# FNet + PEER kernel: the first stage ordered by hand and pinned, query weights loaded first, the column-257 sums on GpSimd, six statistics on ScalarE

## The chip, the cores and the metric

The kernel runs on one core of one Trainium2 chip. The time is that of the device in microseconds (us), from the runs of the whole program. Matrix work is done by TensorE (PE); VectorE (DVE), ScalarE (ACT) and GpSimd (POOL) work on arrays; SyncE (SP) issues most of the transfers (DMA). Each engine goes through its own list of instructions in order and waits at an instruction until what it needs is there.

## The reference

From one array x (2048 rows, 512 columns) and its normalised rows xn, two things are computed and added to x:

```python
def _A_ref(xn, dft_seq_re, dft_seq_im, dft_hid_re, dft_hid_im):
    a = jnp.einsum("bsd,ed->bse", xn, dft_hid_re)
    b = jnp.einsum("bsd,ed->bse", xn, dft_hid_im)
    return jnp.einsum("ts,bse->bte", dft_seq_re, a) - jnp.einsum("ts,bse->bte", dft_seq_im, b)

def _B_ref(xn, w_q, k1, k2, u, v):        # 32 heads, 64 keys, K = 2, 4096 experts
    q = jnp.einsum("nd,dhc->nhc", xn, w_q)
    s1 = jnp.einsum("nhd,ed->nhe", q[..., :dk], k1)
    s2 = jnp.einsum("nhd,ed->nhe", q[..., dk:], k2)
    ...
    g = _softmax(top_s, axis=-1)
    act = _gelu(jnp.einsum("nd,nhkd->nhk", xn, u[top_e]))
    return jnp.einsum("nhk,nhk,nhkd->nd", g, act, v[top_e])

return x + _A_ref(xn, ...) + _B_ref(xn, ...)
```

A is the real part of a Fourier transform over rows and columns. B takes for each row and head the two best of 64 keys from each of two sets, adds their scores in pairs, keeps the best two of the four sums, and adds up the outputs of the experts chosen in this way. All inputs are float32.

## The kernel before

**Tiles and groups.** The 2048 rows are 16 tiles of 128 rows. Four tiles make a group, which `xp[2 * g]` and `xp[2 * g + 1]` hold (128 x 2 x 512 float32 each, half a megabyte); `xn(g, q)` is one tile. A group consists of the rows that the symmetry of the transform brings together. The groups are taken in the order `G = (1, 0, 2, 3)`.

**What the first stage does with a group.** `ln` collects mean and variance of its four tiles, on DVE (L361 and L362, `bn_stats` and `bn_aggr`) or, for two tiles of the second group and one of the fourth, on ACT with two instructions (L347, L348). A square root on ACT and five or more small instructions on DVE (L367 and its neighbours) make the scale and the shift; `ln_norm` applies them, two tiles on DVE (L313), two on ACT (L386). `fold(k, g)` then adds (k = 0, for the cosines) or subtracts (k = 1, sines) mirrored halves: one instruction over 1024 columns (L416), then some of 254 to 257 columns (L397, L400, L405 to L407, L419, L420), all on DVE but the copy L405. The result, 2 x 257 columns, is `Q[k][g]`. `main(k, g)` multiplies it on PE by the table `A[k, g]` that `load(k, g)` brought (L449, eight records of 512 columns in float32), and adds the four groups up in four banks of PSUM. `stage(i)` splits a normalised tile into a high half on ACT (L521) and a low half on DVE (L522), both 16 bits wide, and SP transposes them by DMA (L523) for the scores.

**Query weights.** The scores need products of the query weights with the keys. The heads are worked on in eight chunks. For a chunk, `m_load` loads four tiles of weights, `m_mul(j, t, kds)` multiplies them by the keys on PE (L152, 64 columns wide), and `m_parts` splits the result for 16-bit products (ACT L226, DVE L227). For the first chunk the scale comes from sums over the weights and keys (`w_sums`, ACT L209 and the next, then one product by ones on PE, then `w_scale`). `early(n)` computes the scores of the first eight tiles for the first chunk inside the first stage (PE L252, 12 products of 512 columns each, ACT L285 takes them out of PSUM).

**What the tiles leave over.** Column 257 of the folded arrays does not fit into the 256 columns of the products. `sides` adds up these parts for all groups on DVE, with one fused multiplication and addition each (L454, L456, L477) at the end of the stage. `fold_row` folds the one row that stands alone, on POOL (L425, then L397 to L407 on one partition); `spread` and `evict` bring the results out of PSUM.

**Order.** The kernel is written as a program in one order, and a planner sorts the instructions of each engine by its own estimates, so that instructions of later work can be put ahead. An instruction given to `tc.keep_in_program_order` stays behind the one that its engine had before it in the text. Nothing in the first stage of this kernel is pinned. `heat(n)` puts n products of ones on PE which nobody uses (L555). `behind_stage` writes one column of a buffer on POOL from a staged tile, so that the load into that buffer waits for that tile (L587). Loads of x, of the tables, of weights and the transposes are issued from SP; `c5s`, `c5r`, `c55` and `x5`, all small, from ACT. The transfers are told apart by eight counters in turn, so the ninth waits for the first.

**Behind the first stage** come the sums over the parts left over (`sums`, POOL L825 to L833, `hid` with POOL L540 and L541), the weights of the next chunks, which `m_prep` splits (ACT L162, POOL L166 and L167), the scores of all tiles, the routing on DVE and POOL, and the experts (PE L1103), which take most of the time.

## Time and profile before

| | |
|---|---|
| median of three runs (lowest, highest) | 1115.78 us (1115.4, 1116.73) |
| profiled execution, its time | 1117.59 us |
| its span, first to last instruction | 1115.7 us |
| mean granted clock of PE | 0.996 |
| PE busy | 1102.7 us, 99% of the span |
| PE loading weights | 721.8 us, 65% |
| DVE busy | 937.7 us, 84% |
| ACT busy | 695.8 us, 62% |
| POOL busy | 333.4 us, 30% |
| instructions | 29227 |

The profile comes from one execution of the program. An engine's time counts as busy while it executes an array instruction; weight loads run beside the products and are counted by themselves. `L152` is line 152 of the kernel. A group of instructions is named by line, engine, operation and tile (`m<-k_sb,wq`: from `k_sb` and `wq` into `m`), with its partitions and elements, its type and count, then the busy time in us, the mean duration of one in ns, and the idle time just before them with what ended it. In the timeline a row has its start in us, its duration in us, then the instruction; a bracket gives how long the engine had waited and for what; `x24` joins so many of a kind in one row. The first stage lasts until about 77 us.

### The profile page before, as it was taken

How to read it: one execution, taken by the hardware profiler on the slowest of the kernel's cores; microseconds unless marked ns; L12 is line 12 of the kernel's file. 1: busy time of each engine (PE TensorE's matmuls, PEld its weight loads, DVE VectorE, ACT ScalarE, POOL GpSimd, SP SyncE). 2: the span in 40 equal slices, each digit the busy share in tenths (PEclk: the TensorE clock that was granted, in tenths of full speed). 3: DMA queues.
4: the chain of work that ended last, by engine and by line, in shares of the span. 5: the costliest groups of instructions: out<-in, count | busy, mean ns of one | idle time of the engine just before them, and what ended most of it. 6: DMA issues, size and time to landing. Idle time of an engine off the chain costs nothing.

```text
span 1115.7 us, 29227 instructions
## 1 busy us (share of the span) xinstructions
PE 1102.7 (99%) x11528; PEld 721.8 (65%) x11528; DVE 937.7 (84%) x2828; ACT 695.8 (62%) x1238; POOL 333.4 (30%) x385
## 2 busy tenths in 40 slices
PE   9999999999999999999999999999999999999997
PEld 6465554545445449877677677677677677677643
DVE  7899698999999899697797797699699599599790
ACT  6557598988887666355665666565657566566520
POOL 1519999898888861000000000000000000000000
PEclk8999999999999999999999999999999999999999
DMA  8885456464362353587678677677768867866433
GB/s 285 259 216 189 133 197 203 139 205 136 114 199 80 101 140 110 168 259 274 242 237 294 236 254 270 228 244 256 255 224 270 300 221 236 294 204 218 134 105 117
DMA packets 134866, 229.96 MB, mean 206 GB/s; under 512 B 35380, under 2 KB 71355, under 8 KB 134718
## 3 DMA queue, kind: packets, MB, share of 16 engines
q1 hardware_dynamic: 132112, 223.72, 60.1%
q0 software_dynamic: 2304, 4.20, 2.2%
q8 instruction: 92, 1.51, 0.6%
q14 instruction: 56, 0.46, 0.1%
q10 hardware_dynamic: 302, 0.08, 0.0%
HBM read 192.49 MB, written 29.69 MB: 199 GB/s over the span
## 4 chain that ended last, share of the span: by engine, by line
PE 80%; DVE 7%; POOL 6%; DMA 3%; ACT 2%; issue 1%; SPq 0%; POOLq 0%; ACTq 0%; DVEq 0%
PE z L1103 27%; PE v L1103 27%; PE s L252 19%; PE g L1103 4%; PE m L148 1%; POOL v L795 1%; DVE L L1098 1%; DVE vals L972 1%; PE m L152 1%; PE p L449 1%; DVE idx L976 1%; DVE g L1098 1%; DMA xt_d<-xq 1%; POOL u L540 1%; POOL v L825 1%
## 5 line engine op out<-in xcount | busy, mean ns | idle before, releaser
L252 PE MATMUL s<-m,xq 128*128 128x512 f16 x1344 | 297.5, 379 | 1.4 <-ACT ss L968 1.4
L1103 PE MATMUL v<-v,act 128*128 128x512 f16 (+1 forms) x1068 | 248.3, 377 | 0.7 <-DVE act L1098 0.7
L252 PEld LDWEIGHTS <-xq 128*128 128x128 f16 x1344 | 129.7, 98 | 152.6 <-issue 2.7
L1385 POOL DMA_DIRECT2D y<-in_x_dram x16 | 14.4, 899 | 647.2 <-DMA y<-y_d 318.4
L1103 PEld LDWEIGHTS <-u 128*128 128x128 f16 x3456 | 198.3, 98 | 14.4
L1103 PEld LDWEIGHTS <-act 128*128 128x128 f16 x1068 | 97.9, 98 | 95.7 <-DVE act L1098 1.2
L1098 DVE TENSOR_TENSOR L<-io_lam,cmp 128x2048 f16<-128x2048 f16 x120 | 144.9, 1220 | 6.9 <-PE g L1103 6.7
L972 DVE MAX8 vals<-ss 128x8 f32<-128x64 f32 x896 | 133.3, 216 | 5.3 <-ACT ss L968 5.1
L1103 PE MATMUL z<-xb,u 128*128 128x128 f16 x2112 | 127.7, 219 | 0.0
L1103 PEld LDWEIGHTS <-s 128*128 128x128 f16 x1944 | 113.4, 98 | 12.5
L1103 PE MATMUL v<-v,w 128*128 128x512 f16 x480 | 113.0, 379 | 0.0
L1098 ACT ACTIVATE cx<-cx 128x896 f32<-128x896 f32 (+2 forms) x134 | 83.5, 625 | 31.7 <-DVE cx L1098 30.3
L968 ACT ACTIVATE ss<-s,wsc 128x512 f32<-128x512 f32 x120 | 80.1, 680 | 22.4 <-PE s L252 12.6
L1098 DVE TENSOR_TENSOR cx<-cx 128x128 f32<-128x128 f32 (+9 forms) x226 | 91.7, 418 | 2.7 <-DMA cx<-in_cb_dram 1.1
L976 DVE FIND_INDEX8 idx<-vals,ss 128x8 uint16<-128x256 f32 x224 | 93.8, 419 | 0.0
L1103 PE MATMUL z<-x,u 128*128 128x128 f16 x1344 | 84.2, 219 | 0.0
L1098 ACT ACTIVATE act<-act,scl 128x512 f32<-128x512 f32 x56 | 40.2, 719 | 66.4 <-DVE act L1098 66.4
L1103 PE MATMUL z<-x,s 128*128 128x128 f16 x1296 | 81.2, 219 | 0.0
L1103 PEld LDWEIGHTS <-L 128*128 128x128 f16 x2048 | 65.0, 96 | 16.1 <-DVE R L1098 0.7
L1098 ACT ACTIVATE act<-g 128x1024 f16<-128x1024 f32 x40 | 51.5, 1311 | 37.3 <-DVE g L1098 36.9
L1098 DVE TENSOR_TENSOR act<-z,act 128x512 f32<-128x512 f32 x44 | 30.4, 690 | 49.7 <-PE z L1103 45.9
L1103 PEld LDWEIGHTS <-w 128*128 128x128 f16 x480 | 43.8, 98 | 43.2
(333 smaller groups left out, 1794.8 us busy)
## 6 DMA issues: line engine op xcount, KB each, us to landing
s<-s_d SPq DMA_DIRECT2D x81, 512.0 KB, 4.4
v<-v_d SPq DMA_DIRECT2D x67, 512.0 KB, 4.7
cx<-in_cb_dram SPq DMA_DIRECT2D x64, 448.0 KB, 5.9
w<-in_wq_dram SPq DMA_DIRECT2D x28, 512.0 KB, 5.9
fit<-in_wq_dram SPq DMA_DIRECT2D x28, 512.0 KB, 5.0
uv<-in_vn_dram SPq DMA_DIRECT2D x16, 512.0 KB
uv<-in_ut_dram SPq DMA_DIRECT2D x16, 512.0 KB, 3.6
s_d<-v SPq DMA_DIRECT2D x32, 256.0 KB, 2.5
```

The source lines that it names most:

```text
L148: nc.tensor.matmul(MS[j, "p"][kd][:, c0:c0 + 64], MS[j, t, "l" if l else "h"][:, hh, kd * P:(kd + 1) * P], k16[:, r, t // 2, :], start=n = ...
L152: nc.tensor.matmul(MS[j, "p"][kd][:, c0:c0 + 64], MS[j, t][:, hh, kd * P:(kd + 1) * P], k_sb[:, t // 2, :], start=True, stop=True)
L252: nc.tensor.matmul(ps, xt[i][:, l, kd, :], m[:, r, kd, :], start=(n == 0), stop=(n == 3 * KD - 1))
L449: nc.tensor.matmul(PP[k][dt][h], l[:, dt * P:(dt + 1) * P], r, start=first, stop=last)
L540: nc.gpsimd.tensor_tensor(t[:, b:513:2], t[:, e], im, op=ALU.add)
L795: nc.gpsimd.tensor_tensor(l, t, h, op=ALU.subtract)
L968: nc.scalar.activation(s, ps, AF.Copy, scale=inv)
L972: nc.vector.max(vals[:, i, w, :, h], s[:, g, :])
L976: nc.vector.max_index(idx[:, i, w].rearrange("p k h -> p (k h)"), vals[:, i, w, 0:2].rearrange("p k h -> p (k h)"), s[:, w * HC:g + 1, :]. ...
L1098: return (lambda *a, **k: pin(f(*a, **k))) if keep_on[0] else f
L1103: i = nc.tensor.matmul(*a, **k)
L1385: pin(nc.gpsimd.dma_start(Y[b], x[b % 4, b // 4], accum_op=ALU.add))
```

## The change

In the first stage every instruction on DVE, ACT, PE and SP is pinned to the order in which the program has it: the four engines are wrapped in `First`, which pins while `keep0[0]` is true, and the stage is written out anew in one order (POOL stays with the planner). Query weights of the first chunk are loaded right behind the first group, their 64 products come ahead of the first `main` (apart from 10 fillers, and after 40 instead of 44 at the start). The statistics of two tiles in each of the second, third and fourth group are taken on ACT: six instead of three. `sides` is taken apart into `side256`, `side5` and `side_rows`, which scale and add on POOL, group by group, with two instructions where DVE had one fused. The four small loads go out from SP instead of ACT; `behind_stage` goes; the copy in the fold (L405) is on DVE for all groups; the second half of the folds goes through the groups in the order (1, 2, 3, 0), and two tiles change places in the order of staging; `k16` is made after the stage. Of the names `dve`, `act`, `syn` and `ten` in place of `nc.vector`, `nc.scalar`, `nc.sync` and `nc.tensor` elsewhere nothing more is shown.

```diff
+    keep0 = [False]
+    class First:
+        def __init__(self, eng):
+            self.eng = eng
+        def __getattr__(self, name):
+            f = getattr(self.eng, name)
+            return (lambda *a, **k: tc.keep_in_program_order(f(*a, **k))) if keep0[0] else f
+    dve, act, syn, ten = First(nc.vector), First(nc.scalar), First(nc.sync), First(nc.tensor)
...
-    GK = G, (0, 1, 2, 3)
-    TO = [4, 5, 6, 7, 0, 1, 8, 9, 2, 3, 10, 11, 12, 13, 14, 15]
+    GK = G, (1, 2, 3, 0)
+    TO = [4, 5, 6, 7, 0, 1, 8, 9, 10, 11, 2, 3, 12, 13, 14, 15]
...
+    def ln_act(g, qs):
+        for q in qs:
             junk = Q[1][g].rearrange("p a d -> p (a d)").bitcast(BF16)[:, 2:514]
-            zero = 0.0
-            if n == 3:
-
-                zero = nm0[:, 0, 0:1]
-                nc.scalar.activation(zero, xn(G[1], 3)[:, 0:1], AF.Copy, scale=0.0)
-            nc.scalar.activation(junk, xn(g, q), AF.Identity, bias=zero, scale=1.0 / 512, accum_out=mvs[:, g, q, 0:1])
-            nc.scalar.activation(junk, xn(g, q), AF.Square, bias=mvs[:, g, q, 0:1], scale=-1.0,
-                                 accum_out=mvs[:, g, q, 1:2])
-        if onact:
-            v = mvs[:, g, 0:len(onact), 1]
-            nc.scalar.activation(v, v, AF.Copy, scale=1.0 / 512)
-        for q in range(4):
-            if q in onact:
-                continue
-            if n == 0:
-                st = da.tile([P, 6], F32, tag="st", name=f"st{g}_{q}", bufs=2)
-            else:
-                c = NW + 12 * (n % 2) + 6 * (q % 2)
-                st = fits[:, c:c + 6]
-            nc.vector.bn_stats(st, xn(g, q))
-            nc.vector.bn_aggr(mvs[:, g, q, :], st)
+            act.activation(junk, xn(g, q), AF.Identity, bias=0.0, scale=1.0 / 512, accum_out=mvs[:, g, q, 0:1])
+            act.activation(junk, xn(g, q), AF.Square, bias=mvs[:, g, q, 0:1], scale=-1.0,
+                           accum_out=mvs[:, g, q, 1:2])
+        if 1 in qs:
+            v = mvs[:, g, 0:2, 1]
+            act.activation(v, v, AF.Copy, scale=1.0 / 512)
...
+    def ln_dve(g, q):
+        n = G.index(g)
+        if n == 0:
+            st = da.tile([P, 6], F32, tag="st", name=f"st{g}_{q}", bufs=2)
+        else:
+            c = NW + 12 * (n % 2) + 6 * (q % 2)
+            st = fits[:, c:c + 6]
+        dve.bn_stats(st, xn(g, q))
+        dve.bn_aggr(mvs[:, g, q, :], st)
+    def ln_end(g, between=()):
         var = mvs[:, g, :, 1]
         sm = da.tile([P, 3, 4], F32, tag="sm", name=f"sm{g}", bufs=2)
+        act.activation(sm[:, 0], var, AF.Sqrt, bias=eps)
+        for f in between:
+            f()
+        dve.reciprocal(sm[:, 1], sm[:, 0])
...
-            if e is nc.gpsimd or first:
-                e.tensor_copy(f[:, :, 0:P + 1:P], t[:, :, 255:257])
-            else:
-                nc.scalar.activation(f[:, :, 0:P + 1:P], t[:, :, 255:257], AF.Copy)
+            e.tensor_copy(f[:, :, 0:P + 1:P], t[:, :, 255:257])
...
+    def fold_x(k, g):
+        FF["t"] = da.tile([P, 2, 512], F32, tag="ft", name=f"ft{k}_{g}", bufs=1)
+        dve.tensor_tensor(FF["t"], xp[2 * g], xp[2 * g + 1], op=ALU.subtract if k else ALU.add)
+    def fold_q(k, g):
         f = da.tile([P, 2, 256], F32, tag="ff", name=f"ff{k}_{g}", bufs=2)
-        o = FF[k, g] = da.tile([P, 2, 257], F32, tag="fo", name=f"fo{k}_{g}", bufs=2)
+        o = da.tile([P, 2, 257], F32, tag="fo", name=f"fo{k}_{g}", bufs=2)
-        nc.vector.tensor_tensor(t, xp[2 * g], xp[2 * g + 1], op=op)
-        fold_d(k, t, f, o, first=G.index(g) == 1)
+        fold_d(k, FF["t"], f, o)
...
-    def add(dst, a, v, first=False):
-
-        if first:
-            nc.vector.tensor_scalar(dst, v, a, None, op0=ALU.mult)
-        else:
-            nc.vector.scalar_tensor_tensor(dst, v, a, dst, op0=ALU.mult, op1=ALU.add)
...
+    def side256(n):
+        g = G[n]
+        t = (s256, a256, a256, t256)[n]
+        for h in range(2):
+            nc.gpsimd.tensor_scalar(t[:, h], A[0, g][:, h * 512:(h + 1) * 512], Q[0][g][:, h, 256:257], None,
+                                    op0=ALU.mult)
+        if n in (1, 2):
+            nc.gpsimd.tensor_tensor(s256, s256, t, op=ALU.add)
+        if n == 3:
             for h in range(2):
-                a, v = Q[0][g][:, h, 256:257] if n else f[:, h:h + 1], A[0, g][:, h * 512:(h + 1) * 512]
-                if n < 3:
-                    add(s256[:, h], a, v, n == 0)
-                    continue
                 for q in range(2):
-                    nc.vector.scalar_tensor_tensor(turned(a256[:, h])[:, :, q], halved(v)[:, :, q], a,
-                                                   halved(s256[:, h])[:, :, q], op0=ALU.mult, op1=ALU.add)
-        for n, g in enumerate(G):
-            for k in range(2):
-                add(a5[:, k, :257 - k], c5s[:, k, g:g + 1] if n else f[:, 2 + k:3 + k],
-                    Q[k][g][:, k, :257 - k], n == 0)
+                    nc.gpsimd.tensor_tensor(turned(a256[:, h])[:, :, q], halved(s256[:, h])[:, :, q],
+                                            halved(t[:, h])[:, :, q], op=ALU.add)
+    def side5(k, n):
+        g = GK[k][n]
+        c = slice(0, 257 - k)
+        t = t5[:, c] if n else a5[:, k, c]
+        nc.gpsimd.tensor_scalar(t, Q[k][g][:, k, c], c5s[:, k, g:g + 1], None, op0=ALU.mult)
+        if n:
+            nc.gpsimd.tensor_tensor(a5[:, k, c], a5[:, k, c], t, op=ALU.add)
+    def side_rows():
         r = da.tile([1, 1, 1024], F32, tag="r5", name="r256", bufs=1).rearrange("p o (a t) -> p (o a) t", a=2)
-        nc.scalar.activation(turned(r[:, 0]), halved(c5r), AF.Identity, bias=zs[0:1, 2:3], scale=s5[:, 256:257])
-        nc.scalar.activation(r[:, 1, 0:257], s5, AF.Identity, bias=zs[0:1, 2:3], scale=c55)
-        nc.vector.tensor_tensor(a256[0:1, 0], a256[0:1, 0], r[:, 0], op=ALU.add)
-        nc.vector.tensor_tensor(a5[0:1, 0], a5[0:1, 0], r[:, 1, 0:257], op=ALU.add)
+        act.activation(turned(r[:, 0]), halved(c5r), AF.Identity, bias=zs[0:1, 2:3], scale=s5[:, 256:257])
+        act.activation(r[:, 1, 0:257], s5, AF.Identity, bias=zs[0:1, 2:3], scale=c55)
+        nc.gpsimd.tensor_tensor(a256[0:1, 0], a256[0:1, 0], r[:, 0], op=ALU.add)
+        nc.gpsimd.tensor_tensor(a5[0:1, 0], a5[0:1, 0], r[:, 1, 0:257], op=ALU.add)
...
-    s256, a256 = [uf[i].rearrange("p (h t) -> p h t", h=2) for i in (0, 2)]
+    s256, a256, t256 = [uf[i].rearrange("p (h t) -> p h t", h=2) for i in (0, 2, 7)]
+    t5 = uf[1][:, 640:897]
...
+    def stage_tile(i):
+        n = TO.index(i)
+        return u_sb[SB[n] // 2][:, SB[n] % 2].rearrange("p a k n -> p a (k n)")
+    def stage_hi(i):
+        act.activation(stage_tile(i)[:, 0], xn(i // 4, i % 4), AF.Identity,
+                       bias=zs[:, 2:3] if TO.index(i) > 7 else zs[:, 0:1])
+    def stage_lo(i):
+        t = stage_tile(i)
+        dve.tensor_tensor(t[:, 1], xn(i // 4, i % 4), t[:, 0], op=ALU.subtract)
+        syn.dma_start_transpose(xt[i].rearrange("p a k n -> p (a k) n"), t.rearrange("p a d -> p (a d)"))
+    def stage(i):
+        stage_hi(i)
+        stage_lo(i)
...
-    heat(44)
-    load_x(G[0])
-    load(0, G[0])
-    w_load((0, 1))
-    load_x(G[1])
-    w_load((2, 3))
-    load_x(G[2])
...
-    def behind_stage(t):
-        nc.gpsimd.tensor_copy(t[:, 0:1], last[:, 0:1])
-    for g in G[1:3]:
-        load(0, g, behind_stage)
-    for h in range(2):
-        behind_stage(xp[2 * G[3] + h][:, 0])
-    load(0, G[3], behind_stage)
-    ln(G[1], 1)
...
+    keep0[0] = True
+    heat(40)
+    load_x(G[0])
+    w_load(range(4))
+    load(0, G[0])
+    load_x(G[1])
+    load_x(G[2], (0,))
+    syn.dma_start(c5s, c5)
+    row512(0, c5r)
+    syn.dma_start(c55, cb[0, 0, 0, 0:1, 8, 0:1])
+    syn.dma_start(x5, x[2:4, 0, 0:1].rearrange("q p d -> p q d"))
     nc.gpsimd.tensor_copy(c52, c5r[:, 0:2])
+    m_mul(0, 0, ALL)
+    for q in range(4):
+        ln_dve(G[0], q)
+    ln_end(G[0])
     wtot = pa("wsum")
+    ten.matmul(wtot[:, 0:2], ones, w_sums(), start=True, stop=True)
+    ln_norm(G[0], (0, 2))
+    w_scale(wtot, 1e-13)
+    for t in range(1, 4):
+        m_mul(0, t, ALL)
+    ln_norm(G[0], (1, 3))
+    fold_x(0, G[0])
+    for i in TO[0:4]:
+        stage_hi(i)
+    fold_q(0, G[0])
+    heat(10)
+    main(0, G[0])
+    stage_lo(TO[0])
+    stage_lo(TO[1])
+    m_parts(0, MS[0, "p"])
+    ln_act(G[1], (0, 1))
+    stage_lo(TO[2])
+    stage_lo(TO[3])
+    load_x(G[2], (1,))
+    load(0, G[1])
     load_x(G[3])
+    load(0, G[2])
+    ln_dve(G[1], 2)
+    ln_dve(G[1], 3)
+    ln_end(G[1])
+    ln_norm(G[1], (0, 2, 1, 3))
+    for i in TO[4:6]:
+        stage_hi(i)
+    early(0)
+    fold_x(0, G[1])
+    early(1)
+    for i in TO[4:6]:
+        stage_lo(i)
+    ln_act(G[2], (0, 1))
+    early(2)
+    side256(0)
+    side5(0, 0)
+    fold_q(0, G[1])
+    early(3)
     main(0, G[1])
+    load(0, G[3])
+    ln_dve(G[2], 2)
+    ln_dve(G[2], 3)
+    ln_end(G[2], [lambda: ln_dve(G[3], 2)])
+    ln_norm(G[2], (0, 2, 1, 3))
     for i in TO[6:8]:
+        stage_hi(i)
+    ln_dve(G[3], 3)
+    fold_x(0, G[2])
+    for i in TO[6:8]:
+        stage_lo(i)
+    ln_act(G[3], (0, 1))
+    early(4)
+    fold_q(0, G[2])
+    side256(1)
+    side5(0, 1)
     def w4_part(t):
+        return wq_view(t, w4)
+    for n, h in enumerate(GK[1]):
+        load(1, h)
+        m_load(1, w4_part, (n,))
         if h == 0:
             row512(1, A[1, 0][0:1, 512:1024])
+    syn.dma_start(wfs, wf)
+    syn.dma_start(w2, wr[:, 0:2].to_broadcast([P, 2]))
+    ln_end(G[3])
+    ln_norm(G[3], (0, 2, 1, 3))
+    fold_x(0, G[3])
+    early(5)
+    main(0, G[2])
+    side256(2)
+    side5(0, 2)
+    act.activation(nm5, negm[0:1, 0, 2:4], AF.Identity, bias=zs[0:1, 3:4])
+    for q in range(2):
+        act.activation(x5[:, q], x5[:, q], AF.Identity, bias=nm5[:, q:q + 1], scale=rstd[0:1, 0, q + 2:q + 3])
+    early(6)
+    early(7)
+    fold_q(0, G[3])
     fold_row(0)
     fold_row(1)
     main(0, G[3])
     spread()
     evict(0)
+    side256(3)
+    side5(0, 3)
     M[1] = MP[1].tile([P, 2, KD, 512], F16, tag="m", name="m1"), inv1
     MS[1, "s"] = sm0
     m_mul(1, 0, range(KD))
+    for n, g in enumerate(GK[1]):
         if g == 0:
+            for i in TO[8:10]:
+                stage(i)
+        fold_x(1, g)
+        fold_q(1, g)
+        if g == 0:
+            dve.tensor_copy(Q[1][0][0:1, 0, 1:256], s5i[:, 1:256])
+            act.activation(xp[1][0:1], x5, AF.Copy)
+        side5(1, n)
         main(1, g)
+        if n < 2:
+            m_mul(1, n + 1, range(KD))
     m_mul(1, 3, range(KD))
+    for i in TO[10:]:
         stage(i)
+    side_rows()
+    evict(1)
     m_parts(1, MS[1, "p"])
+    keep0[0] = False
+    act.activation(k16[:, 0], k_sb, AF.Copy, scale=sk)
+    dve.scalar_tensor_tensor(k16[:, 1], k_sb, sk, k16[:, 0], op0=ALU.mult, op1=ALU.subtract)
```

235 lines of the change are left out of this document (76 added, 159 removed).

## The prediction

> **What bounds the kernel now.** I read the busy time by stage first, then the timeline of TensorE (PE), then the granted clock, then VectorE (DVE) and GpSimd (POOL) side by side. By stage (length, then busy time and count of PE, weight loads, DVE, ScalarE (ACT), POOL, then clock, DMA share, GB/s):
>
> ```profile
> 9.48:24.00 14.52, 14.51 (x75) 11.55 (x76) 12.41 (x37) 11.07 (x25) 3.03 (x11) 0.76 0.99 298
> 24.00:57.00 33.00, 32.15 (x128) 14.65 (x127) 28.94 (x70) 19.71 (x40) 14.09 (x19) 1.00 0.84 269
> 57.00:77.50 20.50, 20.50 (x95) 12.86 (x95) 19.94 (x46) 11.52 (x22) 0.00 (x0) 1.00 0.85 208
> 77.50:164.80 87.30, 86.87 (x552) 47.60 (x552) 76.71 (x421) 63.01 (x153) 80.80 (x102) 1.00 0.53 179
> 164.80:1115.70 950.90, 941.37 (x10634) 629.47 (x10633) 795.89 (x2244) 587.27 (x998) 234.97 (x245) 1.00 0.62 204
> ```
>
> PE has work in all of 24 to 1115.7 us but about 11, and the change removes none of it. So the end moves by what PE gains or loses in the first stage, which ends at 77.5, as long as POOL (80.8 of 87.3 us busy just behind it) follows. PE in that stage (start, length):
>
> ```profile
> 0.98 7.34 PE L555 MATMUL warm<-ones 128*128 128x256 f16 x50 [0.98 <-POOL ones L86]
> 9.48 3.98 PE L152 MATMUL m<-k_sb,wq 128*128 128x64 f32 x24 [1.16 <-DMA wq<-in_wq_dram]
> 15.41 5.06 PE L449 MATMUL p<-c,q 128*128 128x512 f32 x8
> 20.30 3.68 PE L152 MATMUL m<-k_sb,wq 128*128 128x64 f32 x32
> 23.82 10.52 PE L252 MATMUL s<-m,xq 128*128 128x512 f16 x48
> ...
> 58.39 3.65 PE L449 MATMUL p<-c,q 128*128 128x512 f32 x8
> ...
> 75.75 1.90 PE L152 MATMUL m<-k_sb,w 128*128 128x64 f32 x16
> 77.48 5.34 PE L252 MATMUL s<-m,xq 128*128 128x512 f16 x24
> ```
>
> Filler until 8.3, a wait of 1.16 us for the first query weight, then work without a break. What can be won is the start; what can be lost is anything that makes PE wait for DVE. DVE and POOL together, in the one place of the stage where both have array work:
>
> ```profile
> 47.91 1.27 POOL L425 TENSOR_TENSOR r<-u 1x512 f32<-1x512 f32 x1
> 47.94 1.53 DVE L406 TENSOR_TENSOR fo<-ff 128x254 f32<-128x254 f32 x1
> 49.27 0.69 POOL L397 TENSOR_TENSOR r<-r 1x254 f32<-1x254 f32 x1
> 49.40 0.85 DVE L407 TENSOR_TENSOR fo<-ff 128x254 f32<-128x254 f32 x1
> ...
> 52.70 1.27 POOL L425 TENSOR_TENSOR r<-u 1x512 f32<-1x512 f32 x1
> ...
> 55.20 0.44 POOL L407 TENSOR_TENSOR s5i<-r 1x127 f32<-1x127 f32 x1
> ```
>
> This is the row on which I rest most. A DVE addition of 254 columns takes 1.53 us when a POOL instruction of 1.27 us began 0.03 us before it, and 0.85 beside the next. Undisturbed, the same addition takes 0.42 (next fence). So the two do not run beside each other: each waits for the other's whole instruction, and they take turns.
>
> **The change part by part.** Durations (busy time, mean ns):
>
> ```profile
> L166 POOL TENSOR_SCALAR w<-w,wsc 128x1024 f32<-128x1024 f32 x2 | 5.7, 2846 | 24.6 <-ACT wh L162 24.6
> L167 POOL TENSOR_TENSOR w<-w,wh 128x1024 f16<-128x1024 f32 x24 | 51.1, 2135 | 1.5 <-ACT w L164 1.4
> L833 POOL TENSOR_TENSOR v<-v,v 128x256 f32<-128x256 f32 x7 | 5.1, 726 | 0.5
> L406 DVE TENSOR_TENSOR fo<-ff 128x256 f32<-128x256 f32 x4 | 1.7, 422 | 0.8 <-ACT ff L405 0.8
> L313 DVE TENSOR_SCALAR x<-x,mvs,rstd 128x512 f32<-128x512 f32 x4 | 2.1, 540 | 0.0
> L522 DVE TENSOR_TENSOR u<-xq,u 128x512 f16<-128x512 f32 x8 | 5.1, 684 | 0.6 <-ACT u L521 0.6
> L367 DVE SCALAR_TENSOR_TENSOR sm<-mvs,sm 128x4 f32<-128x4 f32 x4 | 0.6, 156 | 0.1
> L361 DVE BATCH_NORM_STATS2 sums<-xq 128x6 f32<-128x512 f32 x7 | 4.5, 675 | 0.0
> L456 DVE SCALAR_TENSOR_TENSOR u<-c,q,u 128x512 f32<-128x512 f32 x4 | 2.9, 745 | 0.0
> 57.26 1.22 DVE L416 TENSOR_TENSOR ft<-x,xq 128x1024 f32<-128x1024 f32 x1
> 60.45 1.22 DVE L416 TENSOR_TENSOR ft<-xq,xq 128x1024 f32<-128x1024 f32 x1
> ```
>
> *Sums of column 257, DVE to POOL.* One fused DVE instruction (745 ns for 512 columns) becomes a scaling and an addition on POOL. By proportion from L166, scaling 512 columns is 1.42 us and 257 columns 0.71; an addition of 256 or 257 is 0.73 (L833), of 1024 2.13 (L167). The fixed part of an instruction makes the proportion a lower end, by some 0.1 each. For the second and third group: 2 x 1.42 + 2.13 + 0.71 + 0.73 = 6.4 us each; for the fourth 2 x 1.42 + 4 x 0.73 + 0.71 + 0.73 = 7.2; for the second half's first three folds 0.71 + 2 x 1.44 = 3.6. The row sums that POOL does already cost 2.94 us each (52.70 to 55.64, with DVE idle), so 5.9. POOL thus has 6.4 + 6.4 + 7.2 + 3.6 + 5.9 = 29.5 us to do between the moment the second group's fold is ready and the last fold.
>
> The Trainium skill, GPSIMD Engine Reference, section 4.1 Engine selection, says that one-input instructions on GpSimd run at roughly line rate. The row disagrees: one input (L166) costs more than two (L167). With the page's 128 elements a cycle at 1.2 GHz, scaling 512 columns would be an estimated 0.43 us, scaling 257 an estimated 0.21; six of each make 8.9 us less, and the forecast below would be +7.4 us. The row decides.
>
> *What DVE does in that time.* A fold takes 3.2 us (57.26 to 60.45), and six remain: 19.2. Four normalisations (L313) 2.1, four low halves for staging (L522) 2.6, eight small steps of the statistics (L367 and its like) 1.3: 25.2 us. All of these are of the kinds that read arrays as the delayed additions do; that L313 with its one array waits too I take from its nearest kin; without it 2.1 falls away. The statistics (L361) I count at nothing: one input, and I let POOL run beside them.
>
> *The sum.* In the kernel before, the second group's fold is done at 32.6, and DVE stands still once, for POOL's row sums:
>
> ```profile
> 32.16 0.42 DVE L420 TENSOR_TENSOR q<-fo 128x257 f32<-128x257 f32 x1
> ...
> 55.67 0.28 DVE L655 COPY q<-s5i 1x255 f32<-1x255 f32 x1 [3.37 <-POOL s5i L407]
> ```
>
> The hand order has m_parts wait for all 64 query products, the stage halves behind it, but fewer statistics ahead: between 32.6 and 34.5; I take 33.5. The stand of 3.37 us goes, since group 0 now comes last in the second half; DVE is then late by its turns instead. If DVE and POOL alternate from there with no time in which neither works (in which order the planner puts POOL's work does not matter for that), the last fold ends at 33.5 + 29.5 + 25.2 = 88.2. Behind it PE still has a main of 3.65 and a query product of 1.90: 93.8, where it was 77.5 (75.75 + 1.90 less the overlap of their ends). That is +16.3 us. Nothing behind takes it back, since PE is full to the end; DVE and POOL come out of the stage about as late as PE. I keep 0 to +3 us more in the range, for the clock (below) drops when PE waits.
>
> *The start.* The first weight is queued behind x alone:
>
> ```profile
> 5.31 1.29 DVE L361 BATCH_NORM_STATS2 st<-x 128x6 f32<-128x512 f32 x2 [4.29 <-DMA x<-in_x_dram]
> ```
>
> The first half megabyte has landed at 5.31, the weight as the fourth at 9.48: 1.39 us each. As the third it lands at 8.1, so products start 1.4 us earlier. Filler stays at 50. The clock in three stretches:
>
> ```profile
> 4.50:11.35 6.85, 5.69 (x51) 5.01 (x49) 4.86 (x16) 4.43 (x8) 0.00 (x0) 1.00 1.01 371
> 11.35:14.76 3.41, 3.40 (x18) 3.27 (x16) 2.60 (x5) 1.71 (x7) 2.37 (x6) 0.50 1.05 415
> 14.76:18.18 3.42, 3.42 (x8) 1.87 (x9) 3.17 (x9) 3.25 (x8) 0.00 (x0) 0.50 0.98 365
> ```
>
> From 11.35 to 14.76 PE is busy all the time with query products, at half clock (18 instructions in 3.41 us against 16 in 1.90 at full clock), and the half clock stays; it goes only after 512-column products from 15.41. The change puts 48 query products in one row there, with nothing wide between. I expect them all at half clock, about 0.21 instead of 0.12 us: +4 us, which eats the 1.4. In the forecast this hides under the DVE and POOL sum; with that cover gone it is the second rival.
>
> *Costed at nothing:* six statistics on ACT instead of three (19.71 of 33.00 busy from 24 to 57), three small copies on DVE that were ACT's, four small DMA issues from the ACT to the SP queue (ten half megabytes are ahead of them, 5.31 + 9 x 1.39 = 17.8 us, and only POOL waits for them), loads that no longer wait for casts on POOL, k16 later (used from the third chunk of heads on). What covers them is PE's backlog; if it is gone, the longest is the ACT queue, where the square root of a group sits behind evictions: up to 2 us.
>
> **Rivals.**
>
> *DVE keeps the shared path, POOL is late (+10, 1126 us).* For it, this row: a cast of one column that waited through eight DVE instructions.
>
> ```profile
> 41.23 3.46 POOL L587 CAST c<-u 128x1 f32<-128x1 f16 x1 [20.76 <-PE s L252]
> ...
> POOL w L166 <- ACT wh L162: 24.6, 1, 24.6
> ...
> 164.83 0.22 PE L148 MATMUL m<-sums,wh 128*128 128x64 f16 x2 [0.46 <-ACT u L537]
> ```
>
> Against it, the turns at 47.9. DVE would be through at about 65 (33.5 + 25.2 + four statistics at 0.85 + some 3 of waits for ACT, an estimate). POOL would get what DVE leaves until then, say 8 of its 36.5 us (29.5 + 3.6 for the first group + 3.4 for the last sums), and end at 93.5. Its next work, which ACT releases at 80.2 after 24.6 us without any, is 13 late. Up to 164.8 POOL has 6.5 us of idle time at most, and PE there already waits 0.46 for what POOL and ACT prepare: between +7 and +13, I take +10.
>
> *Only the clock (+2.4, 1118 us).* No collision reaches PE. It waits once, for the sums of the scales:
>
> ```profile
> 11.03 1.04 ACT L209 ACTIVATE m<-wq 128x1024 f16<-128x1024 f32 x1
> ```
>
> This can begin when the weight is there and the first root is out, at 8.6; with the second sum and two short steps about 1 us more, so 10.6. PE's own sum: 10.6, then 48 products 5.7 at full clock, 10 fillers 1.1, eight mains 29.2, eight early scores 20.8 (10.52 for four, less the tail), four query products 7.4, the spread 0.6: 75.4 with full clock, 79.9 with half clock for the 48. It decides if the folds are in time and the clock is as from 11.35.
>
> *Faster (-2.5, 1113 us).* The mechanism is the same sum at full clock, 75.4 less about 0.4 of overlapping ends, against 77.5. Its place is 8 to 24 us, its price 48 x 0.09; it decides once the last fold is ready by 70 and the granted clock is 1.0 through the query products. For it: DVE is rid of the fused sums (L456 alone 2.9 us) and of three statistics. Against it: the half-clock row, and 29.5 + 25.2 us of turns. The Trainium skill, TensorE: Matmul & The Clock Gate, Part 1, lets the clock rise after one busy window of about 3.4 us; by that rule the 48 products would run at full clock. This trace does not agree for narrow products: 3.40 busy of 3.41 us, and no rise.
>
> **How the numbers follow.** Profiled execution: 1117.59 us with a span of 1115.7, so 1.9 lie around it; the median shown is 1115.78, and I add the change of the span to the median: 1115.78 + 16.3 = 1132. Chances: forecast 0.47, POOL late 0.14, clock alone 0.12, faster 0.27, for offloading is a gain wherever the turns turn out milder than two rows tell. 0.2% (2.2 us) is about what a measurement of this kernel can tell from nothing. Of the faster case, whose time may be 0 to 5 us less, 0.18 lies beyond 2.2 us and 0.09 within; of clock alone (+0.5 to +4) 0.07 is slower and 0.05 within. Faster 0.18, same 0.14, slower 0.47 + 0.14 + 0.07 = 0.68. The forecast's own range is 1125 to 1138: low end with the scalings cheaper or DVE's waits overlapping, high end with 0.1 more per POOL instruction and the clock. The range for all reaches from 1112 to 1138.
>
> **What would show it.** Right: the fold additions that take 0.42 now average over 1 us; POOL is busy from the second group's fold on almost without a break until 90; the last query product of the stage ends near 94; the clock is 0.5 for at least 7 us after 11. Wrong: fold additions at 0.42 beside POOL work of 128 rows; the first score after the stage before 80; POOL scalings of 512 columns under 1 us.

## The result, and the profile after

The changed kernel took 1124.64 us in the median (1124.13 to 1124.98, six runs), the kernel before 1115.64 on the same chip (1115.19 to 1117.94, six runs): 1.007 of its time, 95% interval 1.006 to 1.008. It is slower, as forecast, but by 9.0 us and not by 16.3. The profiled execution took 1124.64 us with a span of 1122.8, where that of before had 1117.59 and 1115.7: +7.1 us, which is what the traces can explain, for the profiled execution of before lay 1.9 us above the median of its runs. Two executions of the experiments, one of the kernel before at 3643 us and one of e5 at 2299 us, are left out below.

By stage, for the changed kernel (length, then busy time and count of TensorE (PE), weight loads, VectorE (DVE), ScalarE (ACT), GpSimd (POOL), then granted clock, DMA share, GB/s):

```profile
24.00:57.00 33.00, 30.21 (x107) 12.62 (x104) 31.64 (x63) 20.23 (x41) 22.59 (x17) 0.95 1.01 317
57.00:77.50 20.50, 18.23 (x77) 11.23 (x77) 20.26 (x29) 7.25 (x14) 18.57 (x19) 0.92 0.37 99
77.50:90.00 12.50, 12.50 (x63) 7.09 (x62) 7.97 (x24) 10.03 (x18) 8.70 (x5) 1.00 1.03 196
```

PE stood 0.85 us in all of this time before; now it stands 2.8 of 33 and 2.3 of 20.5 us, and its clock falls in both stretches. Its timeline in the changed kernel (start, length; L83 is the wrapper through which every pinned instruction goes):

```profile
8.69 1.97 PE L83 MATMUL m<-k_sb,wq 128*128 128x64 f32 x16 [0.76 <-DMA wq<-in_wq_dram]
...
10.69 5.55 PE L83 MATMUL m<-k_sb,wq 128*128 128x64 f32 x48
...
20.61 10.53 PE L83 MATMUL s<-m,xq 128*128 128x512 f16 x48
...
42.70 5.40 PE L83 MATMUL p<-c,q 128*128 128x512 f32 x8 [2.61 <-DVE q L83]
...
67.15 5.40 PE L83 MATMUL p<-c,q 128*128 128x512 f32 x8 [1.80 <-DVE q L83]
...
81.04 1.90 PE L83 MATMUL m<-k_sb,w 128*128 128x64 f32 x16
...
172.75 0.22 PE L161 MATMUL m<-sums,wh 128*128 128x64 f16 x2 [0.56 <-ACT u L552]
```

The first score begins at 20.61, where it began at 23.82 with the same products and fillers ahead of it: the start won 3.2 us. Then PE waits three times (2.61 and 1.80 us for a fold, and 0.47 for ACT ahead of 59.95), and the `main` behind each long wait takes 5.40 us in place of 3.6 to 3.7, for its clock is at half. From the first score to the last query product it is 60.4 us instead of 51.9 in the kernel before, 8.5 more: 4.0 of waits (4.9 less the 0.85 of before), 3.5 of half clock, and about 1 because, by their rows, products behind a wait don't overlap with the ends of those before them. Net of the 3.2 us won, the last query product starts at 81.04 instead of 75.75: +5.3. And PE's wait for products of the third chunk, which ended at 164.83, now ends at 172.75: +7.9. So 2.6 us more are lost behind the stage, where I had expected nothing; 2.0 of them are three waits for ACT's evictions of scores (`ss`) between 142 and 150 us.

What holds the folds up, in the timelines of DVE and POOL in the changed kernel:

```profile
61.94 3.02 DVE L83 TENSOR_TENSOR fo<-ft 128x2 f32<-128x2 f32 x1
62.03 0.71 POOL L477 TENSOR_TENSOR u<-u,u 128x256 f32<-128x256 f32 x1
62.72 0.44 POOL L415 TENSOR_TENSOR s5i<-r 1x127 f32<-1x127 f32 x1
63.13 0.44 POOL L416 TENSOR_TENSOR s5i<-r 1x127 f32<-1x127 f32 x1
63.53 2.33 POOL L477 TENSOR_TENSOR u<-u,u 128x256 f32<-128x256 f32 x3
...
77.16 3.68 DVE L83 TENSOR_TENSOR u<-xq,u 128x512 f16<-128x512 f32 x6
77.21 4.42 POOL L485 TENSOR_SCALAR u<-q,c5s 128x256 f32<-128x256 f32 x1 [1.58 <-DVE q L83]
```

A DVE addition of two columns, 0.15 us undisturbed, takes 3.02: it waits through five POOL additions in a row. At 77.21 it is the other way: a POOL scaling that takes 0.92 us elsewhere (in e3, at 84.92) takes 4.42, through six DVE instructions. In these rows the one waits for the other, but they don't take turns one by one, as I had read the two rows of before: here the one that has work queued without a gap keeps going.

Behind the stage, ACT and POOL in the changed kernel, and below them the same two steps in the kernel before:

```profile
81.90 0.60 ACT L83 ACTIVATE u<-p 128x512 f32<-128x512 f32 x1 [1.67 <-DMA xq<-u]
...
84.50 2.43 ACT L83 ACTIVATE m<-m,wsc 128x512 f16<-128x512 f32 x4
...
88.06 2.93 POOL L179 TENSOR_SCALAR w<-w,wsc 128x1024 f32<-128x1024 f32 x1 [3.72 <-ACT wh L175]
```
```profile
76.45 2.42 ACT L226 ACTIVATE m<-m,wsc 128x512 f16<-128x512 f32 x4
...
80.20 2.85 POOL L166 TENSOR_SCALAR w<-w,wsc 128x1024 f32<-128x1024 f32 x1 [24.56 <-ACT wh L162]
```

POOL's first work on the weights of the third chunk starts 7.86 us later. From there to the end of PE's wait it is 84.7 us in the changed kernel (172.75 - 88.06) and 84.6 in the kernel before (164.83 - 80.20). I read this as the chain which ends last, and it has moved by more than PE has.

### The profile page after: what moved, and what is told of

Its sections match the earlier page's. It is cut to its first block, busy times and chain, and to the rows that moved or that the text cites. A ratio compares the mean times of both kernels' runs of the same rounds, so it can differ in the third digit from the quotient of the medians.

```text
span 1122.8 us, 29213 instructions
## 1 busy us (share of the span) xinstructions
PE 1104.8 (98%) x11528; PEld 720.4 (64%) x11528; DVE 943.4 (84%) x2802; ACT 696.2 (62%) x1242; POOL 371.7 (33%) x403
## 4 chain that ended last, share of the span: by engine, by line
PE 77%; DVE 4%; ACT 2%; POOL 1%; issue 1%; DMA 0%; ACTq 0%
PE z L1143 27%; PE v L1143 27%; PE s L265 18%; PE g L1143 4%; PE m L161 1%; DVE L L1138 1%; DVE g L1138 1%; DVE R L1138 1%; DVE act L1138 0%; DMA s_d<-v 0%; POOL u L822 0%; POOL v L835 0%; ACT u L550 0%; ACT uv L821 0%; ACT ss L1008 0%
## 5 line engine op out<-in xcount | busy, mean ns | idle before, releaser
L265 PE MATMUL s<-m,xq 128*128 128x512 f16 x1272 | 282.1, 380 | 3.4 <-ACT ss L1008 3.4
L265 PEld LDWEIGHTS <-xq 128*128 128x128 f16 x1272 | 122.6, 98 | 146.6 <-issue 5.2
L1016 DVE FIND_INDEX8 idx<-vals,ss 128x8 uint16<-128x256 f32 x224 | 93.8, 419 | 0.0
L1138 DVE TENSOR_TENSOR act<-z,act 128x512 f32<-128x512 f32 x44 | 30.3, 688 | 49.6 <-PE z L1143 45.9
L1143 PEld LDWEIGHTS <-w 128*128 128x128 f16 x480 | 43.7, 98 | 43.2
```

Of the source, the lines that this page charges most:

```text
L265: ten.matmul(ps, xt[i][:, l, kd, :], m[:, r, kd, :], start=(n == 0), stop=(n == 3 * KD - 1))
L1016: nc.vector.max_index(idx[:, i, w].rearrange("p k h -> p (k h)"), vals[:, i, w, 0:2].rearrange("p k h -> p (k h)"), s[:, w * HC:g + 1, :]. ...
L1138: return (lambda *a, **k: pin(f(*a, **k))) if keep_on[0] else f
L1143: i = nc.tensor.matmul(*a, **k)
```

## The experiments

Times are read against the kernel before on the same chip, which took 1117.57, 1117.38, 1116.36 and 1117.04 us in the median beside e1 to e4, e5 to e8, e9 to e11 and e12, and 1116.8 in the one execution beside e13 and e14. One kernel's executions differ by some us (more on this at the end). Edits are shortened.

**e1: the sums back on DVE, at the very end.**

```diff
-    side256(n), side5(k, n)      # POOL, group by group
-    side_rows()
     evict(1)
     m_parts(1, MS[1, "p"])
+    sides()                      # DVE, fused, as before
```

> The changed kernel with the sums of column 257 back on VectorE as fused instructions, all at the end of the stage. Theory A (the GpSimd sums and VectorE's additions hold each other up): the folds no longer wait, TensorE has no wait of 2.6 and 1.8 us for them and keeps its clock, the first score after the stage starts at 74 to 76 instead of 82.8, and the time is 1112 to 1115 us. Theory B (the pinned order is what costs): the waits for folds stay, the time is 1120 us or more.

Measured: 1132.62 us, 1.0139 of before (1.0122 to 1.0157). TensorE, ACT and POOL:

```profile
71.56 1.89 PE L83 MATMUL m<-k_sb,w 128*128 128x64 f32 x16
...
86.68 2.19 ACT L175 ACTIVATE wh<-w,u 128x1024 f16<-128x1024 f32 x2 [9.05 <-DVE u L83]
87.94 2.85 POOL L179 TENSOR_SCALAR w<-w,wsc 128x1024 f32<-128x1024 f32 x1 [33.02 <-ACT wh L175]
```

Both theories miss. The stage on PE ends as early as theory A says: the last query product starts at 71.56, 9.5 us earlier than in the changed kernel and 4.2 earlier than before, and the waits for folds are gone but for 0.29 us. But the time is the worst so far. The sums now stand on DVE from 77.7 to 86.6, and ACT waits 9.05 us for them before POOL can start, at 87.94, as late as in the changed kernel (88.06). That an early PE is worth little when POOL starts late brought up the theory of the chain. It doesn't explain why e1 is 8 us slower than the changed kernel. Those are lost later:

```profile
145.53 14.45 PE L265 MATMUL s<-m,xq 128*128 128x512 f16 x60 [11.93 <-ACT ss L1000]
```

ACT had waited 13.58 us there for POOL, and POOL 7.49 for a transfer. Why this transfer came late is open.

**e2: no sums.** Calls of `side256` and `side5` removed, `a256` and `uf[1]` set to zero at the start.

> The changed kernel without the sums of column 257 of x over the groups (the arrays are set to zero instead, so this part of the transform is left out). It gives the price of all GpSimd side work. Theory A: the stage ends at 73.5 to 75.5 and the time is 1111 to 1114 us, at most 2 us below the run with the sums on VectorE. Theory B: 1120 us or more.

Measured: 1115.98 us, 0.9993 of before (0.9975 to 1.0012). TensorE and POOL:

```profile
72.66 1.89 PE L83 MATMUL m<-k_sb,w 128*128 128x64 f32 x16
...
78.98 2.86 POOL L179 TENSOR_SCALAR w<-w,wsc 128x1024 f32<-128x1024 f32 x1 [7.18 <-ACT wh L175]
...
163.65 0.22 PE L161 MATMUL m<-sums,wh 128*128 128x64 f16 x2 [0.58 <-ACT u L554]
```

Without POOL's sums the whole loss is gone, and theory B with it: the price of the sums is about 9 us, and the rest of the change costs nothing that outweighs its gain. (DVE is rid of its sums here as well; e5, which has them, is the like-for-like comparison.) But PE's stage ends 3.1 us earlier than before (72.66 against 75.75) and of this only 1.2 are left at 163.65: from POOL's start it is 84.7 us again.

**e3: only the sums moved to POOL, the rest as before.**

```diff
-    sides()
+    side256(n), side5(k, n)      # POOL, at the same places as in the change
+    side_rows()
```

> The kernel before with only the sums of column 257 moved to GpSimd at the same places; the planner orders the rest as it likes. Theory A: VectorE's fold additions are stretched here too, the folds become late, the time is 5 to 12 us above the kernel before. Theory B: within 2 us of the kernel before.

Measured: 1126.27 us, 1.0076 of before (1.0057 to 1.0095). TensorE, ACT and POOL:

```profile
81.02 1.89 PE L152 MATMUL m<-k_sb,w 128*128 128x64 f32 x16
...
88.57 1.15 ACT L162 ACTIVATE wh<-w,u 128x1024 f16<-128x1024 f32 x1 [1.56 <-POOL u L486]
89.82 2.84 POOL L166 TENSOR_SCALAR w<-w,wsc 128x1024 f32<-128x1024 f32 x1 [1.28 <-ACT wh L162]
```

The one part does all of it, and with the planner's order as much as with the pinned one (+8.7 us). POOL's start is late in another way here: ACT, and POOL behind it, wait for the last of POOL's own sums, which end at 88.5.

**e4: the kernel before with 56 fillers.** `heat(44)` becomes `heat(56)`.

> The kernel before with 56 instead of 44 products of filler at the start, so that TensorE doesn't wait 1.16 us for the first query weight. Theory C (the wait made the clock fall to half in the next stretch of 3.41 us): the granted clock stays 1.0 from the start, the 24 and 32 query products take 0.12 us each, and the time falls by 2.5 to 3.5 us to 1112 to 1113. Theory D (64-column products can't hold the clock, as the forecast had it): the clock is 0.5 somewhere from 11 to 18 us all the same, the time stays within 1 us of before.

Measured: 1116.75 us, 0.9996 of before (0.9987 to 1.0006). The stretch in which the query products run, then TensorE and POOL:

```profile
9.47:12.88 3.41, 3.41 (x33) 3.30 (x31) 2.67 (x6) 2.15 (x7) 0.52 (x3) 1.00 1.04 400
```
```profile
73.54 1.89 PE L152 MATMUL m<-k_sb,w 128*128 128x64 f32 x16
...
79.33 2.85 POOL L166 TENSOR_SCALAR w<-w,wsc 128x1024 f32<-128x1024 f32 x1 [25.89 <-ACT wh L162]
...
163.98 0.22 PE L148 MATMUL m<-sums,wh 128*128 128x64 f16 x2 [0.57 <-ACT u L537]
```

Theory C is right on the clock: with no wait it stays at 1.00 through the query products (33 instructions in a stretch, six of them fillers, where before had 18 at 0.50). It is wrong on the time: PE is 2.2 us ahead at the end of the stage and 0.85 at 163.98, again 84.65 us behind POOL's start. Nor do the fillers beat every execution of the kernel before: its eight with a mean clock of 0.998 or more had a median span of 1114.25 us beside e4's 1114.9.

**e5: the sums on DVE, ahead of the eviction.** As e1, with `sides()` in the place of `side_rows()`.

> The changed kernel with the sums of column 257 on VectorE again, now ahead of the eviction and of the query products' split, where VectorE had stood still. Theory E (behind the stage GpSimd's own chain sets the end: TensorE's wait for products of the third chunk came 84.1 us behind GpSimd's first scaling of query weights in the kernels before and after and in three experiments): TensorE's stage ends at 73 to 75 instead of 77.4 (kernel before), GpSimd's first scaling starts at 79 to 80, so the span is 1114.5 to 1116 us and the time equals the kernel before within 1.5 us. Theory F (TensorE's stage end alone sets the end): the span falls with the stage end to 1111 to 1112 us.

Measured: 1116.68 us, 0.9986 of before (0.9974 to 0.9998). The time is as theory E says; of the stage's end it doesn't tell, since this profiled execution took 1121.72 us, 5 us more than the median, with a low clock at the start:

```profile
7.54:10.95 3.41, 2.68 (x24) 2.71 (x25) 2.17 (x10) 2.24 (x7) 0.00 (x0) 1.00 1.01 404
10.95:14.36 3.41, 3.41 (x18) 3.41 (x18) 2.77 (x10) 3.41 (x6) 1.16 (x3) 0.50 1.03 396
14.36:17.77 3.41, 3.41 (x18) 3.41 (x18) 2.67 (x6) 0.28 (x2) 0.57 (x4) 0.50 0.50 176
```
```profile
10.27 9.87 PE L83 MATMUL m<-k_sb,wq 128*128 128x64 f32 x48
```

The same 48 query products that took 5.55 us in the changed kernel take 9.87 here, at half clock, behind a wait of 1.23 us for the weight in place of 0.76.

**e6, e7, e8: POOL's two scalings of query weights on ACT**, in the changed kernel (e6), in the kernel before (e7), in the kernel before with 56 fillers (e8).

```diff
-        if t > 1 or j > 2:
-            nc.scalar.activation(raw, raw, AF.Copy, scale=at)
-        else:
-            nc.gpsimd.tensor_scalar(raw, raw, sw, None, op0=ALU.mult)
+        nc.scalar.activation(raw, raw, AF.Copy, scale=at)
```

> The changed kernel with GpSimd's two scalings of query weights (2.85 us each, the first and third instruction of its chain behind the stage) done by ScalarE. Theory E: the chain is 5.7 us shorter and no longer ends last; what stays is the later stage end of TensorE (82.7 against 77.4), so the span falls from 1122.8 to 1119.5 to 1121.5 us. Theory F: the span stays at 1122 to 1123.5 us.

> The kernel before with the same two scalings on ScalarE. Theory E: TensorE is full there anyway; its waits of 1.4 and 0.5 us behind the stage go, the span is 1114 to 1115.5 us against 1115.7. Theory F: no change, 1115.2 to 1116.2 us.

> The kernel before with 56 fillers at the start and the two scalings on ScalarE. The fillers alone brought TensorE's stage end from 77.4 to 75.2 and the span only from 1115.7 to 1115.0 us. Theory E: with the shorter GpSimd chain the gain is kept, the span is 1111.5 to 1113.5 us. Theory F: as with the fillers alone, 1114.5 to 1115.5 us.

Measured: e6 1122.30 us, 1.0050 of before (1.0032 to 1.0069); e7 1117.07, 0.9998 (0.9984 to 1.0011); e8 1115.27, 0.9979 (0.9969 to 0.9989). TensorE and POOL in e8:

```profile
73.32 1.89 PE L152 MATMUL m<-k_sb,w 128*128 128x64 f32 x16
...
83.58 4.23 POOL L164 TENSOR_TENSOR w<-w,wh 128x1024 f16<-128x1024 f32 x2 [30.33 <-DMA w<-in_wq_dram]
...
162.58 0.22 PE L148 MATMUL m<-sums,wh 128*128 128x64 f16 x2 [0.56 <-ACT u L534]
```

With the chain shortened, e8 keeps what e4 had to give back: 162.58 - 73.32 = 89.3 us from the last query product to the end of the wait, as in the kernel before (164.83 - 75.75 = 89.1). From POOL's first instruction it is 79.0 us, which is e4's 84.65 less the two scalings, so this doesn't tell whether PE or POOL now ends last. e8 is clearly faster than the kernel before, by 2.1 us in the median; beside those eleven executions of before whose mean clock was 0.998 or more, 0.7 us of span are left (1113.4 against 1114.1). e6 is 4.9 us above before where the changed kernel was 9.0: what is left is about the +5.3 of PE's stage. Its profiled execution (span 1123.2) ran at half clock from 10.7 to 24.3 us, so it can't show this by itself; five of the other executions had spans of 1119.4 to 1120.5, as theory E has it, and three, at such a clock, 1123.1 to 1124.6. e7 doesn't tell: its change lies within the interval, as theory E had it for a kernel in which both limits are level.

**e9: e5 with e8's scalings and 48 fillers.**

> The changed kernel with the sums on VectorE ahead of the eviction, the two scalings of query weights on ScalarE and 48 fillers instead of 40 at the start. Theory E with theory C: TensorE doesn't wait at 8 us, the clock stays at 1.0, the stage ends at 73 to 75, GpSimd's chain is 5.7 us shorter, and the span is 1110.5 to 1112.5 us, 3 to 5 below the kernel before on the same chip. If another chain behind the stage (VectorE's maxima) takes over, 1112.5 to 1114.5 us.

Measured: 1115.14 us, 0.9996 of before (0.9981 to 1.0011). Its executions fall in two groups: nine with spans of 1112.0 to 1113.6 and a clock of 0.999, three with 1118.2 to 1118.9 and 0.993. With 48 fillers a wait of 0.4 us for the weight stays, and the clock falls now and then all the same. The nine lie on both sides of 1112.5, the bound between the two cases that I had named, so which chain ends last in them isn't told. Their median span is 1112.9 us, and 1114.2 for the ten executions of the kernel before with 0.998 or more: with the sums on DVE and the scalings on ACT, the pinned order gains about 1.3 us where the clock holds.

**e10, e11: one kind of POOL's instructions at a time.** e10 leaves out the additions, e11 cuts the scalings to one column.

> The changed kernel with GpSimd's scalings for column 257 but without the additions that follow them (the sums are left incomplete). Theory X (the forecast's: VectorE is held up for as long as a GpSimd array instruction of 128 rows runs, scalings too): VectorE's instructions are stretched by 10 us or more between 30 and 77 us, against about 14 in the changed kernel, and TensorE's stage ends at 79 or later. Theory Y (a scaling, with one array as input, holds VectorE up for about a third of its time): 3 to 6 us of stretch, the stage ends at 74 to 77.

> The changed kernel with GpSimd's additions for column 257 at their full size and the scalings ahead of them cut to one column (the sums are not formed). Theory X: the additions are some 14 of 34 us of GpSimd's work there, so VectorE's stretch is 5 to 7 us. Theory Y: the additions hold VectorE up for all their time and make most of the stretch, 7 to 10 us; the stage ends later than with the scalings alone.

Measured, one execution each: 1118.30 and 1126.34 us. I read them by the 60 instructions of DVE that make the eight folds, as count times mean over the ten groups of their kinds. In the changed kernel three of the groups, and two in e2:

```profile
L83 DVE TENSOR_TENSOR ff<-ft 128x508 f32<-128x508 f32 x8 | 7.0, 872 | 0.2
L83 DVE TENSOR_TENSOR fo<-ft 128x2 f32<-128x2 f32 x8 | 6.3, 786 | 0.0
...
L83 DVE TENSOR_TENSOR fo<-ff 128x254 f32<-128x254 f32 x8 | 4.9, 656 | 0.0
```
```profile
L83 DVE TENSOR_TENSOR ff<-ft 128x508 f32<-128x508 f32 x8 | 5.8, 719 | 0.2
...
L83 DVE TENSOR_TENSOR fo<-ft 128x2 f32<-128x2 f32 x8 | 1.5, 186 | 0.0
```

Together they take 44.1 us in the changed kernel and 35.2 in e2: 8.9 us of waiting. With the scalings alone it is 36.5 (+1.3), with the additions alone 38.0 (+2.8); both theories had expected more of both (their figures were for all of DVE's instructions). e10's last query product starts at 73.08, as theory Y has it; e11's at 80.59 can't be set beside it, since its 48 query products ran at half clock (9.93 us). The two runs point to theory Y but don't add up to 8.9, so both kinds were doubled next.

**e13, e14: scalings issued twice, additions issued twice.**

```diff
-        for h in range(2):
+        for h in (0, 0, 1, 1):
             nc.gpsimd.tensor_scalar(t[:, h], A[0, g]...      # likewise in side5
```
```diff
             nc.gpsimd.tensor_tensor(s256, s256, t, op=ALU.add)
+            nc.gpsimd.tensor_tensor(t, s256, t, op=ALU.add)  # likewise the others
```

> The changed kernel with each of GpSimd's scalings for column 257 issued twice (the same result). The 60 fold instructions of VectorE took 44.1 us in the changed kernel, 35.2 without GpSimd's sums, 36.5 with the scalings alone. Theory X (a scaling holds VectorE up for its whole time): the fold instructions take 5 us more than 44.1 or over. Theory Y (for a small part): at most 3 us more. Under both GpSimd gets some 20 us more work, so its chain starts late and the time rises by 5 to 20 us.

> The changed kernel with each of GpSimd's additions for column 257 issued twice (the second goes into a buffer that the next scaling overwrites). Theory X: some 12 us more work for GpSimd, fold instructions 3 us more than 44.1, less than in the run with scalings twice. Theory Y (additions, with two arrays as input, are what holds VectorE up): the fold instructions take 4 to 9 us more, more than in the run with scalings twice, though GpSimd's added work is less.

Measured, one execution each: 1137.71 and 1133.36 us, with the kernel before at 1116.8. Groups of POOL and DVE with the scalings twice (e13), then of DVE with the additions twice (e14):

```profile
L470 POOL TENSOR_SCALAR u<-c,q 128x512 f32<-128x512 f32 x14 | 25.1, 1802 | 10.6 <-DVE q L83 10.6
```
```profile
L83 DVE TENSOR_TENSOR fo<-ft 128x2 f32<-128x2 f32 x8 | 1.9, 237 | 0.0
```
```profile
L83 DVE TENSOR_TENSOR fo<-ft 128x2 f32<-128x2 f32 x8 | 7.2, 896 | 0.0
```

With some 21 us more of scalings the folds take 43.2 us, 0.9 less than in the changed kernel; with the additions twice they take 48.5, 4.4 more. This total alone is not clean: some 13 of the 21 us fall into the time of the folds, the rest behind it, and three additions move behind it as well. Single rows of e13 show it directly:

```profile
39.68 2.52 POOL L473 TENSOR_TENSOR u<-u,u 128x1024 f32<-128x1024 f32 x1
39.91 2.57 DVE L83 TENSOR_SCALAR xq<-xq,mvs,rstd 128x512 f32<-128x512 f32 x1
...
48.26 7.17 POOL L470 TENSOR_SCALAR u<-c,q 128x512 f32<-128x512 f32 x4 [3.26 <-DVE q L83]
```

Beside one POOL addition of 2.52 us a DVE instruction of 0.54 us takes 2.57, 2.0 longer. Beside four POOL scalings in a row (7.17 us) DVE goes through a whole fold and the small steps ahead of it (48.41 to 55.96), and its rows add up to about 1.8 us more than undisturbed. So it is above all POOL's additions of two arrays that hold DVE up; a scaling of one array does so for a small part of its time. The Trainium skill, SBUF — State Buffer, "Who interferes with whom", says that a VectorE instruction with two inputs in SBUF contends with a GpSimd instruction that reads SBUF, and calls the port pair that they share an exclusive lock. For the additions these runs agree (3.02 us behind five of them); for the scalings, which read SBUF too, they agree only in part: about 1.8 us lost beside 7.17. The long times of e13 and e14 come from POOL itself, whose start behind the stage moves to 101.5 and 96.7 us, behind its own sums as in e3.

**e12: the second eviction freed from the transposes.**

```diff
-    SB = (6, 7, 8, 20, 21, 22, 23, 6, 7, 8, 20, 21, 6, 7, 8, 29)
+    SB = (6, 7, 8, 20, 21, 22, 23, 6, 7, 8, 14, 15, 6, 7, 8, 29)
```

> The changed kernel with two of the staged tiles in another buffer, so that the second eviction, pinned behind the staging, doesn't wait for the transposes that read the buffer into which it writes (ScalarE waited 1.67 us for them at 81.9). Theory G (behind the stage the pinned order delays GpSimd's chain beyond the delay of TensorE: its first scaling comes 5.1 us behind TensorE's last query product, against 2.55 in the kernel before): the eviction starts at about 80.3, the query products' split at 82.5 to 83.2 instead of 84.5, GpSimd's first scaling at 86 to 87 instead of 88.1, and the time is 1 to 2 us below the changed kernel. Theory H (only the lateness of TensorE's stage counts): no change of more than 0.5 us.

Measured: 1124.00 us (1122.50 to 1124.98), 1.0060 of before (1.0043 to 1.0077). ACT, POOL and TensorE:

```profile
79.84 2.00 ACT L83 ACTIVATE u<-p 128x512 f32<-128x512 f32 x4
81.75 2.37 ACT L83 ACTIVATE m<-m,wsc 128x512 f16<-128x512 f32 x4
...
85.28 2.87 POOL L179 TENSOR_SCALAR w<-w,wsc 128x1024 f32<-128x1024 f32 x1 [1.28 <-ACT wh L175]
...
170.01 0.22 PE L161 MATMUL m<-sums,wh 128*128 128x64 f16 x2 [0.57 <-ACT u L552]
```

The eviction starts at 79.84 in place of 81.90, POOL 2.8 us earlier, and PE's wait ends 2.7 us earlier: the mechanism of theory G is there, though 0.8 of it comes with PE, whose last query product starts at 80.28 in place of 81.04. POOL's own sums end at 84.00 here, just as ACT is done with the split, so no more could be won in this way. In the time it doesn't show clearly; the intervals of this run and of the changed kernel overlap, and the profiled execution lost 2.7 us again at 412 us, where a later wait let its clock fall.

## Why the prediction was wrong, point by point

*What bounds the kernel: half right.* PE is full before the change, and what makes it wait in the stage is DVE. But "POOL follows" hid a second limit. In eleven of the twelve kernels whose scalings are on POOL the wait at 164.83 ends 84.5 to 84.8 us behind POOL's first scaling (before 84.6, changed 84.7, e2 84.7, e3 84.6, e4 84.7, e5 84.5, e10 84.6, e11 84.8, e12 84.7, e13 and e14 84.6; e1 has no such wait); and in none of the fifteen that have it did it end less than 89.0 us behind the start of the last query products. In the kernel before the two are about level, within what the wait of 0.46 us shows. So a gain at the start seems to need both, and a loss to come from whichever is later; that PE's 89 us are a limit of their own no run isolates.

*The sum, 29.5 + 25.2 us of turns: the step that failed.* It said that all of POOL's work keeps DVE out, so that the last fold would end at 88.2. It ended at 77.0. POOL's work was larger than I had it, not smaller (a scaling of 512 columns takes 1.6 us, the first two 3.21, where I had 1.42), but the folds lost 8.9 us to it, not 29.5. The term mis-sized is above all the scalings: I priced them at their full length on the shared path, 12.8 of the 29.5, and e10 and e13 put them at a small part of that. What remains, the additions and row sums, holds DVE up, as the row at 47.94 had shown, but by less than its length. One by one in turn they did not go. The end at 77.0 hides a second error, which partly cancelled the first: from the second group's fold to the last DVE took 34.9 us in e2, where no sums stand against it and only the row sums are left, and I had 25.2, with its statistics at nothing. In the changed kernel it took 45.9 (31.2 to 77.0). So the sums cost DVE 11.0 us in all, where 23.6 of my 29.5 were theirs.

*No time in which neither works, then PE at 93.8: wrong with it.* PE's stage ended at 82.9 (81.04 + 1.90) and not 93.8: +5.3 and not +16.3.

*"Nothing behind takes it back; DVE and POOL come out about as late as PE": wrong.* POOL's first scaling came 7.9 us late, 2.6 more than PE. I had costed the order at nothing, with up to 2 us for ACT's queue if its cover was gone. There it was: the eviction, pinned behind six stagings, waits 1.67 us for transposes that read its target, and the split of the query products behind it starts 8.05 us late (84.50 against 76.45). e12 gives about 2 us of POOL's start back by a buffer, beside the 0.8 that PE was earlier.

*The start: right in its sign.* I had 1.4 us earlier products and 4 us lost to the clock. The first product starts 0.8 us earlier (8.69 against 9.48), and the 48 products ran at full clock in this execution: 5.55 us. At half clock, as I had forecast, they ran in e5, in 9.87. Narrow products alone don't lower the clock: in the changed kernel a whole stretch of them ran at 1.00, and the clock stayed there.

```profile
5.95:9.37 3.42, 2.66 (x24) 2.23 (x23) 2.81 (x12) 1.09 (x2) 0.00 (x0) 1.00 0.99 374
12.78:16.19 3.41, 3.41 (x33) 3.40 (x32) 3.31 (x9) 3.38 (x7) 2.18 (x6) 1.00 0.96 359
```

What goes ahead of a fall is a longer wait where they begin, and then they keep the clock down (e5: two stretches full of them at 0.50, and the next). The start thus won 3.2 us, which covered part of the loss; that the wait was 0.76 us in this execution, and not longer as in e5, is luck that the forecast had no part in.

*Rivals.* The direction was forecast with 0.68 and came. "DVE keeps the shared path, POOL is late" (1126 us, 0.14) came nearest in time and had the right end, POOL's chain. Its ground is wrong for the changed kernel, where POOL is late by ACT's order and not by its own leftover work, which had ended at 84.3 us; in e3, with the planner's order, that leftover work is the ground. "Only the clock" (1118) and "faster" (1113) fell with the waits for folds.

*What would show it.* Fold additions of 254 columns average 0.66 us (forecast over 1); POOL is busy from 30.9 to 84.3 with two breaks of 3.3 and 1.6 us (forecast until 90); the last query product ends at 82.9 (forecast near 94); a clock of 0.5 for 7 us after 11 is absent here and there in e5.

## What to carry to other kernels

Before work is moved to GpSimd beside VectorE, ask which of its instructions read two arrays: here these held VectorE's additions up, while a scaling of one array cost it little. Before a stage is shortened, follow the work of the other engines behind it to the next wait of the bounding engine; here two chains were about level at 164.8 us, and of 2.2 and 3.1 us won on TensorE (e4, e2) 0.9 and 1.2 were left; with GpSimd's chain shortened as well, all of it was kept (e8). An order pinned by hand fixes also which waits stand ahead of others on a queue, and such a wait may cost at the far end of the queue, not where it stands.
